# Decode attention over a key and value cache: scores of both batches in one group of products, keys loaded a head ahead of values

## The chip, the core and the metric

The kernel runs on one core of a Trainium2 chip. The core has a matrix engine (TensorE, PE in the profile, with PEld for its weight loads), a vector engine (VectorE, DVE), an activation engine (ScalarE, ACT), GpSimd (POOL) and a sync engine (SyncE, SP), which issues every DMA of this kernel. Each engine takes its own instructions in order, and engines wait for one another through semaphores. The metric is the device time of one execution in microseconds (us). Lower is better.

## The reference, cut to what matters

A transformer block decodes one token for each of two batches, with `D` = 512. Everything is float32. The attention reads only the last 4096 rows of a cache of 32768; eight key and value heads serve 32 query heads, four to a head.

```python
def _A_ref(x, k_cache, v_cache, wq, wo):          # x (2, 1, 512); caches (2, 8, 32768, 128)
    W = min(4096, max(256, Sk // 4))              # 4096
    q = (x @ wq).reshape(B, Sq, Hq, Dh).transpose(0, 2, 1, 3)
    k = repeat(k_cache[:, :, Sk - W:, :], 4, axis=1)
    v = repeat(v_cache[:, :, Sk - W:, :], 4, axis=1)
    scores = einsum("bhqd,bhkd->bhqk", q, k) * Dh ** -0.5
    p = softmax(scores)
    o = einsum("bhqk,bhkd->bhqd", p, v)
    return o.transpose(0, 2, 1, 3).reshape(B, Sq, Hq * Dh) @ wo

def reference(...):
    sa, ca, ga, sb, cb, gb = silu(c) @ w_mod, cut in six
    h = layernorm(x) * (1 + ca) + sa
    x = x + ga * _A_ref(h, A_k_cache, A_v_cache, A_wq, A_wo)
    h = layernorm(x) * (1 + cb) + sb
    x = x + gb * (silu(h @ w1) @ w2)              # w1 (512, 1792), w2 (1792, 512)
```

## The kernel before, in words

All large inputs come in through one ring of eight tiles of 128 x 4096 floats (`RING = 8`, `stream`). A load can be issued once the tile eight loads earlier has been read for the last time. The loads stand on SP's queue in program order: `w_mod` (4 loads), `wq` (4), then for each of eight heads the keys of both batches and the values of both batches (`load_k`, `load_v`, 2 MB each), then `wo` (4), `w1` (3) and `w2` (5).

The loop over heads is a software pipeline, and its order is fixed by hand: each instruction in it is wrapped in `inorder`. For head h, VectorE transposes the keys in 32 x 32 blocks, eight instructions, four for each batch (`keys`). TensorE then multiplies the transposed keys by the queries (`scores`). A product here yields 32 rows of the result, so it occupies a strip of 32 of the array's 128 columns, a column group; the four groups are partitions 0, 32, 64 and 96 of the PSUM bank. Batch 0 uses groups 0 and 1, batch 1 uses groups 2 and 3, and the batches are two separate calls. The program shows each float32 product as two instructions in the trace.

Then `maxima` takes the row maxima (VectorE `mx`, a turn on TensorE `mT`, VectorE `mg` and `mrow`), and `exponentials` sends the bias through TensorE (`bp`) and ScalarE (`bias`), and ScalarE computes the exponentials `pr`. `turn` brings the probabilities into the form of weights: VectorE transposes (`xp`) and masks (`zp`), TensorE multiplies by an identity (`pT`), ScalarE copies to `ptb`. `weighted` multiplies them by the values of both batches, sixteen products over four column groups that accumulate in one bank `o`, which ScalarE copies to `ob`. `collect` adds the head's rows to `o_all`.

In the loop (lines 445 to 467), the turn, the values' products and the collection of head h-1 stand inside the iteration of head h: the first key transpose of h, `turn(h-1)`, the rest of batch 0's transposes, `weighted(h-1)`, `scores(h, 0)`, `collect(h-1)`, batch 1's transposes, `scores(h, 1)`, `maxima(h)`, `exponentials(h)`. At the top of iteration h, `fetch(h+1)` issues the two key loads and then the two value loads of head h+1. The buffers for transposed keys (`kT`) are two, one for each batch.

After the loop the attention's result is normalised (`on`, `oq`, `oTn`), multiplied by `wo` (`acc_o` for 24 of 32 slices, `ao` for the last eight), and the second half of the block follows: the layer norm, `hid` with `w1`, the activation up to `uT`, `acc_yw` and `acc_y` with `w2`, `yo`, and the store.

Of the kernel before, what the change touches and what calls it, by code (L numbers as in the profile page):

```python
# [8 lines left out]
F32 = mybir.dt.float32  # L9
# [4 lines left out]
P = 128  # L14
B, D = 2, 512
HQ, HKV, DH = 32, 8, 128
# [7 lines left out]
def adaln_block(  # L24
# [21 lines left out]
    nc = tc.nc  # L46
# [12 lines left out]
    once = ctx.enter_context(tc.tile_pool(name="once", bufs=1))  # L59
# [3 lines left out]
    def const(shape, name):  # L63
        return consts.tile(shape, F32, name=name)

    def bank(tag, name):
        return (psum1 if tag in "CO" else psum).tile([P, 512], F32, tag=tag, name=name)

    def stream(name):
        return ring.tile([P, 4096], F32, tag="st", name=name)  # L70
# [6 lines left out]
    def load_k(b, h):  # L77
        t = stream(f"k{h}_{b}")
        nc.sync.dma_start(
            t, k_cache[b, h, SK - W :, :].rearrange("(p n) d -> p (n d)", p=P)  # L80
        )
        return t

    def load_v(b, h):
        t = stream(f"v{h}_{b}")
        nc.sync.dma_start(
            t, v_cache[b, h, SK - W :, :].rearrange("(p n) d -> p (n d)", p=P)
        )
        return t
# [93 lines left out]
    ptb = [const([P, 17 * 32], f"ptb{i}") for i in range(2)]  # L183
# [4 lines left out]
    qbd = [const([P, 4, B, 4, 32], f"qbd{n}") for n in range(2)]  # L188
# [52 lines left out]
    for k in range(4):  # L241
        ab = wm[k][:, : 2 * D].rearrange("p (s k a c) -> p a s k c", s=2, k=4, a=4)
        cd = wm[k][:, 2 * D :].rearrange("p (s g m) -> p g s m", s=4, g=4)
        for g in range(4):
            r = slice(32 * g, 32 * g + 32)
            nc.tensor.matmul(m_ch[r, :], scT[:, k, :], ab[:, g], start=(k == 0), stop=(k == 3))
        for g in range(4):
            r = slice(32 * g, 32 * g + 32)
# [19 lines left out]
    def turned(t, name):  # L268
        o = const([P, 4, 32], name)
        nc.vector.transpose(o, t.rearrange("p (m k) -> p k m", k=4))  # L270
        return o
# [9 lines left out]
    for k in range(4):  # L281
        wv = wqt[k].rearrange("p (n s g m) -> p n g s m", n=2, s=4, g=G)
        for n in range(2):
            for g in range(G):
# [4 lines left out]
                    start=(k == 0),  # L289
                    stop=(k == 3),  # L290
                )
    for n in range(2):
        qT = once.tile([P, D], F32, tag="wide", name=f"qT{n}").rearrange("p (s j r) -> p s j r", s=4, r=32)
        nc.vector.transpose(qT.rearrange("p s j r -> p (s j r)"), q_ps[n])  # L294
        for g in range(G):
            r = slice(32 * g, 32 * g + 32)
# [8 lines left out]
        for i in range(4):  # L305
            r = slice(32 * i, 32 * i + 32)
# [10 lines left out]

    inorder = tc.keep_in_program_order
    kt, vt, wot, kT = {}, {}, [], {}
    s_ps, mT, pr, o_sb = {}, {}, {}, {}

    def fetch(h):
        for b in range(B):
            kt[h, b] = load_k(b, h)
        for b in range(B):
            vt[h, b] = load_v(b, h)

    def keys(h, b, n4):

        if n4 == 0:
            kT[h, b] = ktp.tile([P, 4, 32, 32], F32, tag="kT", name=f"kT{h}_{b}")
        inorder(nc.vector.transpose(  # L335
            kT[h, b][:, :, 8 * n4 : 8 * n4 + 8, :].rearrange("p j n k -> p n j k"),
            kt[h, b][:, n4 * 1024 : (n4 + 1) * 1024].rearrange("p (n j r) -> p n j r", j=4, r=32),
        ))

    def scores(h, b):  # L340

        if b == 0:
            s_ps[h] = bank("A", f"s{h}")
        for j in range(4):
            for c in range(2):
                r = 64 * b + 32 * c
                inorder(nc.tensor.matmul(  # L347
                    s_ps[h][r : r + 32, :],
                    qbd[h // 4][:, h % 4, b, j, :],
                    kT[h, b][:, j, 16 * c : 16 * c + 16, :],  # L350
                    start=(j == 0),
                    stop=(j == 3),
                ))

    def maxima(h):
        mx = work.tile([P, 1], F32, tag="mx", name=f"mx{h}")
        inorder(nc.vector.tensor_reduce(mx, s_ps[h], axis=AX.X, op=ALU.max))  # L357
        mT = bank("B", f"mT{h}")
        inorder(nc.tensor.matmul(mT[0:1, :P], mx, ident, start=True, stop=True))  # L359
        m = mrow[h % 2]  # L360
        mg = work.tile([1, B, G], F32, tag="mg", name=f"mg{h}")
        inorder(nc.vector.tensor_reduce(
            mg,
            mT[0:1, :P].rearrange("o (b c i g) -> o b g c i", b=B, c=2, g=G)[:, :, :, :, 0:4],
            axis=AX.XY,
            op=ALU.max,
        ))
        inorder(nc.vector.tensor_copy(  # L368
            m.rearrange("o (b c i g) -> o b c i g", b=B, c=2, g=G)[:, :, :, 0:4, :],
            mg[:, :, None, None, :].to_broadcast([1, B, 2, 4, G]),  # L370
        ))

    def exponentials(h):
        bp = bank("B", f"bp{h}")
        inorder(nc.tensor.matmul(bp[:, 0:1], mrow[h % 2], negscale, start=True, stop=True))  # L375
        bias = work.tile([P, 1], F32, tag="bias", name=f"bias{h}")
        inorder(nc.scalar.copy(bias, bp[:, 0:1]))  # L377
        pr[h] = once.tile([P, 16, 32], F32, tag="pr", name=f"pr{h}")
        inorder(nc.scalar.activation(  # L379
            pr[h].rearrange("p s k -> p (s k)"),  # L380
            s_ps[h],
            AF.Exp,
            bias=bias,
            scale=SCALE,
            accum_out=rowsum[:, h : h + 1],
        ))

    def turn(h):

        xp = once.tile([P, 16, 32], F32, tag="xp", name=f"xp{h}")  # L390
        inorder(nc.vector.transpose(xp, pr[h]))  # L391
        zp = once.tile([P, 4, 16, 16], F32, tag="zp", name=f"zp{h}")
        inorder(nc.vector.tensor_mul(  # L393
            zp,
            xp[:, None, :, 0:16].to_broadcast([P, 4, 16, 16]),
            group[:, :, None, None].to_broadcast([P, 4, 16, 16]),
        ))
        tp = bank("C", f"pT{h}")[:, : 2 * P]
        for i in range(4):
            inorder(nc.tensor.matmul(  # L400
                tp[32 * i : 32 * i + 32, :],
                id4,
                zp.rearrange("p a s x -> p (a s) x")[:, :, 4 * i : 4 * i + 4],
                start=True,
                stop=True,
            ))
        inorder(nc.scalar.copy(  # L407
            ptb[h % 2]
            .rearrange("p (b y) -> p b y", b=B)[:, :, :256]
            .rearrange("p b (w z) -> p b w z", z=32)[:, :, :, 0:16],  # L410
            tp.rearrange("p (b w z) -> p b w z", b=B, z=16),
        ))

    def weighted(h):


        o_ps = bank("D", f"o{h}")
        for b in range(B):
            for w in range(8):
                c = w % 4  # L420
                inorder(nc.tensor.matmul(  # L421
                    o_ps[32 * c : 32 * c + 32, :],
                    ptb[h % 2][:, 256 * b + 32 * w : 256 * b + 32 * w + 32],
                    vt[h, b][:, 512 * w : 512 * w + 512],
                    start=(b == 0 and w < 4),
                    stop=(b == 1 and w >= 4),
                ))
        o_sb[h] = once.tile([P, 4 * DH], F32, tag="wide", name=f"ob{h}")
        inorder(nc.scalar.copy(o_sb[h], o_ps))  # L429

    def collect(h):

        for m in range(4):
            r = 64 * (m % 2)
            inorder(nc.tensor.matmul(  # L435
                o_all[r : r + 64, :],
                selh[:, m, HQ - G - G * h : 3 * HQ - G - G * h],
                o_sb[h][:, m * DH : (m + 1) * DH],
                start=(h == 0 and m < 2),
                stop=(h == HKV - 1 and m >= 2),  # L440
                skip_group_check=True,
            ))

    fetch(0)
    for h in range(HKV + 1):
        last, now = h > 0, h < HKV
        if now:
            if h + 1 < HKV:
                fetch(h + 1)
            keys(h, 0, 0)  # L450
        if last:
            turn(h - 1)
        if now:
            for n4 in range(1, 4):
                keys(h, 0, n4)
        if last:
            weighted(h - 1)
        if now:
            scores(h, 0)
        if last:  # L460
            collect(h - 1)
        if now:
            for n4 in range(4):
                keys(h, 1, n4)
            scores(h, 1)
            maxima(h)
            exponentials(h)

    gaT, sbT, cbT = turned(ga, "gaT"), turned(sb, "sbT"), turned(cb1, "cbT")
    nc.vector.tensor_copy(hT[:, :, 1:32:16], sbT[:, :, 0:32:16])  # L470
# [24 lines left out]
    for r in (0, 64):  # L495
# [4 lines left out]
            start=True,  # L500
            stop=True,
# [33 lines left out]
    for q in range(24):  # L535
# [5 lines left out]
            start=(q < 4),  # L541
            stop=(q >= 20),
        )
    for q in range(24, 32):
        for g in range(4):
# [4 lines left out]
                start=(q == 24),  # L550
                stop=(q == 31),
# [24 lines left out]
    for k in range(4):  # L576
        for g in range(4):
# [4 lines left out]
                start=(k == 0),  # L582
                stop=(k == 3),
# [25 lines left out]
    for tt in range(WIDE):  # L609
# [5 lines left out]
            start=(tt < 4),  # L615
            stop=(tt >= WIDE - 4),
        )
    y = bank("D", "acc_y")[:, :P]
    for tt in range(WIDE, T2):
        for g in range(4):  # L620
# [4 lines left out]
                start=(tt == WIDE),  # L625
                stop=(tt == T2 - 1),
# [35 lines left out]
```

## Time and profile before

| What | us |
| --- | --- |
| median of 3 runs | 246.33 (245.33 to 247.42) |
| the profiled execution, its own time | 246.29 |
| its span, first to last instruction | 244.4 |
| PE busy | 165.3 (68%) |
| PEld busy | 47.4 (19%) |
| DVE busy | 114.7 (47%) |
| ACT busy | 25.4 (10%) |
| mean granted TensorE clock | 0.839 |
| moved by DMA | 97.69 MB, mean 400 GB/s |

The profiled execution's own time is 1.89 us more than its span and agrees with the median to 0.04 us. The page cuts the span in 40 slices and gives each engine's busy share, the granted clock (`PEclk`) and the busy share of the 16 DMA engines. The chain of waits goes back from the last instruction, at each step to what released it; its rows are start, duration, engine, tile and line. A window row gives, for a stretch of time, the busy time of each engine, the clock, the DMA share and GB/s. In the timeline `x7` means seven instructions merged into one row. In the groups a line gives the count, busy time, mean ns and what ended the idle time before them.

### The profile page before, as it was taken

Reading aid. Unit: us, or ns where it says so; the run is one execution under the profiler, and the core shown is the slowest. Engines: PE = TensorE matmul, PEld = TensorE weight load, DVE = VectorE, ACT = ScalarE, POOL = GpSimd, SP = SyncE. Lnnn points to the kernel's source line nnn. Section 1 sums busy time; section 2 is a strip of 40 time slices with the busy share of each in tenths; the row PEclk is TensorE's granted clock in tenths of the full one; section 3 lists DMA queues with packets and bytes.
Section 4 is the critical chain, followed back from the end, with each engine's and each line's share of the span. In section 5 each row is a group of like instructions: output and inputs, shape, how many; then the busy total and the mean of one; then the engine's idle time right before and its main releaser. Section 6 shows DMA issues by size and latency. Waiting matters only on the chain.

```text
span 244.4 us, 2546 instructions
## 1 busy us (share of the span) xinstructions
PE 165.3 (68%) x1048; PEld 47.4 (19%) x1048; DVE 114.7 (47%) x176; ACT 25.4 (10%) x56; POOL 10.3 (4%) x30
## 2 busy tenths in 40 slices
PE   0185655295199479749939938974993994769754
PEld 0131001011022012112202202211220221123312
DVE  0724003781691594397089059339708903110230
ACT  2200000101100100010010010001001001001310
POOL 9500001000000000000000000000000000000000
PEclk9999579679569959967985995997798599589979
DMA  6999999999999999999999999999999999999700
GB/s 254 425 432 437 434 426 429 430 429 434 432 429 426 429 429 432 434 429 429 432 432 429 429 437 429 429 434 434 429 432 429 429 425 432 430 416 390 286 3 1
DMA packets 7603, 97.69 MB, mean 400 GB/s; under 512 B 920, under 2 KB 936, under 8 KB 1576
## 3 DMA queue, kind: packets, MB, share of 16 engines
q1 hardware_dynamic: 7592, 97.54, 94.0%
q8 instruction: 8, 0.13, 0.2%
q14 instruction: 3, 0.02, 0.0%
HBM read 97.53 MB, written 0.00 MB: 399 GB/s over the span
## 4 chain that ended last, share of the span: by engine, by line
PE 56%; DMA 24%; DVE 11%; ACT 4%; issue 3%
PE s L347 20%; PE o L421 20%; DMA k<-in_A_k_cache_dram 15%; DMA wq<-in_A_wq_dram 6%; DVE zp L393 4%; PE pT L400 4%; DMA wm<-in_w_mod_dram 3%; DVE xp L391 2%; ACT pr L379 2%; PE acc_o L537 2%; DVE mx L357 2%; PE o_all L435 2%; PE acc_yw L611 1%; PE hid L578 1%; ACT ptb L407 1%
## 5 line engine op out<-in xcount | busy, mean ns | idle before, releaser
L335 DVE STREAM_TRANSPOSE kT<-k 128x1024 f32<-128x1024 f32 x64 | 73.7, 1211 | 3.8 <-DMA k<-in_A_k_cache_dram 3.8
L347 PE MATMUL s<-kT,qbd 128*32 128x512 f32 x256 | 60.6, 604 | 3.8 <-DVE kT L335 3.7
L421 PE MATMUL o<-v,ptb 128*32 128x512 f32 x256 | 47.8, 914 | 3.9 <-ACT ptb L407 3.9
L357 DVE TENSOR_REDUCE mx<-s 128x1 f32<-128x512 f32 x8 | 5.5, 691 | 55.2 <-PE s L347 55.2
L400 PE MATMUL pT<-zp,id 128*32 128x256 f32 x64 | 8.6, 630 | 26.3 <-DVE zp L393 26.3
L347 PEld LDWEIGHTS s<-kT,qbd 128*32 128x32 f32 x256 | 14.2, 111 | 43.0 <-issue 36.4
L421 PEld LDWEIGHTS o<-v,ptb 128*32 128x32 f32 x256 | 10.4, 159 | 41.0 <-issue 30.1
L285 PE MATMUL q<-wq,hq_T 128*32 128x512 f32 x64 | 11.6, 859 | 8.8 <-DMA wq<-in_A_wq_dram 8.8
L393 DVE TENSOR_TENSOR zp<-xp,group 128x1024 f32<-128x1024 f32 x8 | 9.8, 1225 | 0.2
L294 DVE STREAM_TRANSPOSE qT<-q 128x512 f32<-128x512 f32 x2 | 1.4, 718 | 18.1 <-PE q L285 17.8
L429 ACT COPY ob<-o 128x512 f32<-128x512 f32 x8 | 4.7, 585 | 48.9 <-PE o L421 48.9
L377 ACT COPY bias<-bp 128x1 f32<-128x1 f32 x8 | 1.3, 159 | 77.7 <-PE bp L375 77.7
L217 PE MATMUL mean_a<-mv_a,avg 128*128 128x1 f32 x2 | 0.6, 362 | 10.6 <-DVE mv_a L214 10.6
L359 PE MATMUL mT<-ident,mx 128*1 128x128 f32 x16 | 3.0, 270 | 6.3 <-DVE mx L357 6.3
L391 DVE STREAM_TRANSPOSE xp<-pr 128x512 f32<-128x512 f32 x8 | 5.7, 706 | 3.3 <-ACT pr L379 3.3
L400 PEld LDWEIGHTS pT<-zp,id 128*32 128x32 f32 x64 | 1.8, 140 | 26.8 <-issue 25.9
L407 ACT COPY ptb<-pT 128x256 f32<-128x256 f32 x8 | 3.0, 372 | 28.4 <-PE pT L400 28.4
L375 PE MATMUL bp<-negscale,mrow 1*128 1x1 f32 x16 | 3.0, 256 | 4.2 <-DVE mrow L368 4.2
L435 PE MATMUL o_all<-ob,selh 128*64 128x128 f32 x64 | 5.3, 285 | 0.7 <-ACT ob L429 0.7
L285 PEld LDWEIGHTS q<-wq,hq_T 128*32 128x32 f32 x64 | 2.1, 129 | 18.3 <-DMA wq<-in_A_wq_dram 11.2
L537 PE MATMUL acc_o<-wo,oTn 128*32 128x512 f32 x48 | 5.4, 594 | 0.4 <-DVE oTn L515 0.4
L379 ACT ACTIVATE pr<-s,bias 128x512 f32<-128x512 f32 x8 | 5.5, 687 | 0.2
(130 smaller groups left out, 89.7 us busy)
## 6 DMA issues: line engine op xcount, KB each, us to landing
k<-in_A_k_cache_dram SPq DMA_DIRECT2D x16, 2048.0 KB, 31.4
v<-in_A_v_cache_dram SPq DMA_DIRECT2D x16, 2048.0 KB, 23.5
wq<-in_A_wq_dram SPq DMA_DIRECT2D x4, 2048.0 KB
wo<-in_A_wo_dram SPq DMA_DIRECT2D x4, 2048.0 KB, 20.5
wm<-in_w_mod_dram SPq DMA_DIRECT2D x4, 1536.0 KB, 10.2
w<-in_B_w_dram SPq DMA_DIRECT2D x2, 1024.0 KB, 5.9
w<-in_B_w_dram SPq DMA_DIRECT2D x1, 1792.0 KB
w<-in_B_w_dram SPq DMA_DIRECT2D x2, 896.0 KB
```

The source lines that it names most:

```text
L285: nc.tensor.matmul(q_ps[n][32 * g : 32 * g + 32, :], hq_T[:, k, :], wv[:, n, g], start=(k == 0), stop=(k == 3),)
L335: inorder(nc.vector.transpose(kT[h, b][:, :, 8 * n4 : 8 * n4 + 8, :].rearrange("p j n k -> p n j k"), kt[h, b][:, n4 * 1024 : (n4 + 1) * 1 ...
L347: inorder(nc.tensor.matmul(s_ps[h][r : r + 32, :], qbd[h // 4][:, h % 4, b, j, :], kT[h, b][:, j, 16 * c : 16 * c + 16, :], start=(j == 0) ...
L357: inorder(nc.vector.tensor_reduce(mx, s_ps[h], axis=AX.X, op=ALU.max))
L379: inorder(nc.scalar.activation(pr[h].rearrange("p s k -> p (s k)"), s_ps[h], AF.Exp, bias=bias, scale=SCALE, accum_out=rowsum[:, h : h + 1],))
L391: inorder(nc.vector.transpose(xp, pr[h]))
L393: inorder(nc.vector.tensor_mul(zp, xp[:, None, :, 0:16].to_broadcast([P, 4, 16, 16]), group[:, :, None, None].to_broadcast([P, 4, 16, 16]),))
L400: inorder(nc.tensor.matmul(tp[32 * i : 32 * i + 32, :], id4, zp.rearrange("p a s x -> p (a s) x")[:, :, 4 * i : 4 * i + 4], start=True, st ...
L407: inorder(nc.scalar.copy(ptb[h % 2] .rearrange("p (b y) -> p b y", b=B)[:, :, :256] .rearrange("p b (w z) -> p b w z", z=32)[:, :, :, 0:16 ...
L421: inorder(nc.tensor.matmul(o_ps[32 * c : 32 * c + 32, :], ptb[h % 2][:, 256 * b + 32 * w : 256 * b + 32 * w + 32], vt[h, b][:, 512 * w : 5 ...
L435: inorder(nc.tensor.matmul(o_all[r : r + 64, :], selh[:, m, HQ - G - G * h : 3 * HQ - G - G * h], o_sb[h][:, m * DH : (m + 1) * DH], start ...
L537: nc.tensor.matmul(acc[32 * g : 32 * g + 32, :], oTn[:, q, :], wot[q // 8][:, q % 8, :], start=(q < 4), stop=(q >= 20),)
```

## The change

Three things are different.

- `fetch(h)` now issues the keys of head h and the values of head h-1. Keys of head h+1 therefore stand ahead of the values of head h in SP's queue; before the loop only the keys of head 0 are issued, and the last call, `fetch(8)`, issues the values of head 7 alone. The number of loads and their sizes are the same.
- `scores(h)` is one call for both batches, after all eight key transposes. Its loop goes over j, then batch, then half, so four neighbouring products go to four column groups. The products themselves are the same 16.
- `weighted` is called once for each batch. Batch 0's eight products stand ahead of the scores of the next head, batch 1's behind its exponentials. `collect` follows one iteration later, right behind `turn`.

```diff
     def fetch(h):
-        for b in range(B):
-            kt[h, b] = load_k(b, h)
-        for b in range(B):
-            vt[h, b] = load_v(b, h)
+        if h < HKV:
+            for b in range(B):
+                kt[h, b] = load_k(b, h)
+        if h > 0:
+            for b in range(B):
+                vt[h - 1, b] = load_v(b, h - 1)
...
-    def scores(h, b):
-        if b == 0:
-            s_ps[h] = bank("A", f"s{h}")
+    def scores(h):
+        s_ps[h] = bank("A", f"s{h}")
         for j in range(4):
-            for c in range(2):
-                r = 64 * b + 32 * c
+            for b in range(B):
+                for c in range(2):
+                    r = 64 * b + 32 * c
...
-    def weighted(h):
-        o_ps = bank("D", f"o{h}")
-        for b in range(B):
-            for w in range(8):
+    def weighted(h, b):
+        if b == 0:
+            o_ps[h] = bank("D", f"o{h}")
+        for w in range(8):
...
-        o_sb[h] = once.tile([P, 4 * DH], F32, tag="wide", name=f"ob{h}")
-        inorder(nc.scalar.copy(o_sb[h], o_ps))
+        if b == 1:
+            o_sb[h] = once.tile([P, 4 * DH], F32, tag="wide", name=f"ob{h}")
+            inorder(nc.scalar.copy(o_sb[h], o_ps[h]))
...
         if now:
-            if h + 1 < HKV:
-                fetch(h + 1)
+            fetch(h + 1)
             keys(h, 0, 0)
         if last:
             turn(h - 1)
+        if h > 1:
+            collect(h - 2)
+        if last:
+            weighted(h - 1, 0)
         if now:
-            for n4 in range(1, 4):
-                keys(h, 0, n4)
-        if last:
-            weighted(h - 1)
-        if now:
-            scores(h, 0)
-        if last:
-            collect(h - 1)
-        if now:
-            for n4 in range(4):
-                keys(h, 1, n4)
-            scores(h, 1)
+            for n in range(1, 8):
+                keys(h, n // 4, n % 4)
+            scores(h)
             maxima(h)
             exponentials(h)
+        if last:
+            weighted(h - 1, 1)
+    collect(HKV - 1)
```

TensorE's queue before, from the turn of head 1 to the maxima of head 2. `o_467` is the values' sum of head 1, `s_486` the scores of head 2, `kT_0` and `kT_1` the transposed keys of the two batches, `o_all` the collection.

```order
-L400 MATMUL pT_458<-zp_456,id_58 32x256 x4
-L421 MATMUL o_467<-v_0_319,ptb_154 32x512 x8
-L421 MATMUL o_467<-v_1_321,ptb_154 32x512 x8
-L347 MATMUL s_486<-kT_0_452,qbd_159 32x512 x8
-L435 MATMUL o_all<-ob_484,selh 64x128 x4
-L347 MATMUL s_486<-kT_1_499,qbd_159 32x512 x8
-L359 MATMUL mT_514<-ident,mx_512 1x128
```

The same place now: `o_460` is the values' sum of head 1, `s_477` the scores of head 2.

```order
+L402 MATMUL pT_450<-zp_448,id_58 32x256 x4
+L438 MATMUL o_all<-ob_434,selh 64x128 x4
+L423 MATMUL o_460<-v_0_363,ptb_154 32x512 x8
+L349 MATMUL s_477<-kT_0_444,qbd_159 32x512 x2
+L349 MATMUL s_477<-kT_1_472,qbd_159 32x512 x2
...
+L361 MATMUL mT_496<-ident,mx_494 1x128
+L377 MATMUL bp_501<-negscale,mrow_151 128x1
+L423 MATMUL o_460<-v_1_365,ptb_154 32x512 x8
+L402 MATMUL pT_531<-zp_529,id_58 32x256 x4
```

Batch 1's products with the values have moved from ahead of the scores to the place between `bp` and the next `pT`; the collection is that of head 0 and has moved from between the two scores to behind `pT`. The order of VectorE's instructions is unchanged.

SP's queue from the second head's keys on, before and now (the numbers behind the names only tell tiles apart):

```order
 L79 DMA k_0_307<-in_A_k_cache_dram 128x4096
 L79 DMA k_1_309<-in_A_k_cache_dram 128x4096
-L86 DMA v_0_311<-in_A_v_cache_dram 128x4096
-L86 DMA v_1_313<-in_A_v_cache_dram 128x4096
-L79 DMA k_0_315<-in_A_k_cache_dram 128x4096
-L79 DMA k_1_317<-in_A_k_cache_dram 128x4096
...
+L79 DMA k_0_311<-in_A_k_cache_dram 128x4096
+L79 DMA k_1_313<-in_A_k_cache_dram 128x4096
+L86 DMA v_0_315<-in_A_v_cache_dram 128x4096
+L86 DMA v_1_317<-in_A_v_cache_dram 128x4096
```

The first two rows are the keys of head 0. Behind them stood the values of head 0; now the keys of head 1 stand there, and the values of head 0 behind those.

More of the change, by code (lines that the diff above doesn't have):

```diff
@@ L322, in adaln_block @@
     kt, vt, wot, kT = {}, {}, [], {}
-    s_ps, mT, pr, o_sb = {}, {}, {}, {}
+    s_ps, pr, o_ps, o_sb = {}, {}, {}, {}
     def fetch(h):
-        for b in range(B):
-            kt[h, b] = load_k(b, h)
-        for b in range(B):
-            vt[h, b] = load_v(b, h)
+        if h < HKV:
[4 more added lines that the diff above has]
+                vt[h - 1, b] = load_v(b, h - 1)
     def keys(h, b, n4):
@@ L338, in keys @@
         ))
-    def scores(h, b):
-        if b == 0:
-            s_ps[h] = bank("A", f"s{h}")
+    def scores(h):
+        s_ps[h] = bank("A", f"s{h}")
         for j in range(4):
-            for c in range(2):
-                r = 64 * b + 32 * c
[L347 to L353, printed above, removed]
+            for b in range(B):
+                for c in range(2):
+                    r = 64 * b + 32 * c
+                    inorder(nc.tensor.matmul(
+                        s_ps[h][r : r + 32, :],
+                        qbd[h // 4][:, h % 4, b, j, :],
+                        kT[h, b][:, j, 16 * c : 16 * c + 16, :],
+                        start=(j == 0),
+                        stop=(j == 3),
+                    ))
     def maxima(h):
@@ L412, in turn @@
         ))
-    def weighted(h):
-        o_ps = bank("D", f"o{h}")
-        for b in range(B):
-            for w in range(8):
[L420 to L427, printed above, removed]
-        o_sb[h] = once.tile([P, 4 * DH], F32, tag="wide", name=f"ob{h}")
-        inorder(nc.scalar.copy(o_sb[h], o_ps))
+    def weighted(h, b):
+        if b == 0:
+            o_ps[h] = bank("D", f"o{h}")
+        for w in range(8):
+            c = w % 4
+            inorder(nc.tensor.matmul(
+                o_ps[h][32 * c : 32 * c + 32, :],
+                ptb[h % 2][:, 256 * b + 32 * w : 256 * b + 32 * w + 32],
+                vt[h, b][:, 512 * w : 512 * w + 512],
+                start=(b == 0 and w < 4),
+                stop=(b == 1 and w >= 4),
+            ))
+        if b == 1:
+            o_sb[h] = once.tile([P, 4 * DH], F32, tag="wide", name=f"ob{h}")
+            inorder(nc.scalar.copy(o_sb[h], o_ps[h]))
     def collect(h):
```

## The prediction

> **What bounds the kernel now.** I read the page's slices first, then the chain of waits.
>
> ```profile
> DMA  6999999999999999999999999999999999999700
> ```
>
> The DMA engines are full until the 38th of 40 slices (6.1 us each) and then empty while the kernel runs on for two slices and a half. Something other than DMA sets the end. The chain shows what, here one head in its middle, then the end:
>
> ```profile
> 25.79 37.46 DMA k<-in_A_k_cache_dram
> 63.27 1.25 DVE kT L335
> ...
> 183.03 0.70 DVE mx L357
> ...
> 184.69 0.39 PE bp L375 x2
> ...
> 185.29 0.79 ACT pr L379 x2
> 186.10 0.72 DVE xp L391
> 186.85 1.24 DVE zp L393
> 188.22 1.11 PE pT L400 x8
> 189.35 0.38 ACT ptb L407
> 189.78 6.11 PE o L421 x32
> 195.89 3.43 PE s L347 x16
> 199.31 0.59 PE o_all L435 x8
> 199.90 3.58 PE s L347 x16
> 203.50 0.70 DVE mx L357
> ...
> 210.17 6.21 PE o L421 x32
> 216.40 0.59 ACT ob L429
> ...
> 219.93 5.36 PE acc_o L537 x48
> 225.29 0.87 PE ao L546 x32
> ...
> 229.41 1.71 PE hid L578 x16
> ...
> 233.12 2.49 issue
> 235.61 3.56 PE acc_yw L611 x16
> ...
> 240.33 0.70 PE acc_y L621 x24
> ...
> 241.38 0.29 DVE yo L632
> ```
>
> From 63.27, where the first keys of head 1 land, no DMA is on the chain. A head costs 203.50 - 183.03 = 20.47 us, end to end through four engines: 5.06 from `mx` to the end of `zp`, 1.70 to the values' products, 6.11 for them, 7.60 for the scores with the collection between. What does DMA need for a head?
>
> ```profile
> 63.27:222.10 158.83, 118.89 (x668) 32.32 (x672) 88.09 (x100) 14.22 (x37) 0.00 (x0) 0.82 1.01 430
> ```
>
> The last number is 430 GB/s. A key or value load is 4096 x 128 floats, 2.097 MB: 4.88 us each, 19.5 us for a head's four. So the chain falls almost 1 us behind per head, the ring hides it, and the debt comes due at the end. The fifth key or value load landed at 63.27; the last, the 32nd, follows 27 x 4.88 = 131.7 later, at 195.0. Its products start at 210.17, 15 us late, and everything behind them with it.
>
> **The loads.** The change keeps the number and bytes of the loads. Ahead of the last values stand the same 31 loads, so they again land at 195.0. Values of an earlier head land later by two loads, 9.8 us: head 0's at 63.3 and 68.1, where their products before ran from 68.1. At nothing, then, while TensorE arrives no earlier; if it does, it waits, and DMA sets the pace. The ring's part: the loads of head h's values can be issued once batch 1's products of head h-2 are done, later than before, and every later load queues behind them on SP. Eight loads, 39.0 us, lie between the landings of the two; to keep the DMA engines full the issue must come 9.8 us ahead of that for the loads themselves, so 29 us behind the landing of head h-2's values. Even at half clock the products are done 16.4 us behind it (3.6 for batch 0's, 7.1 for the scores, 2.1 from `mx` to the end of `bp`, 3.6 for batch 1's; the rows follow). Some 12 us remain, less the lag. Cost zero; if that cover is gone, each microsecond costs one.
>
> **The head.** What stands between the end of one head's scores and the next? VectorE's order is unchanged, but TensorE's part is not. Values' products of batch 1 leave the stretch from `ptb` to the scores and go behind `bp`; there TensorE had nothing to do until `pT` (185.08 to 188.22), 3.1 us, and the eight products (16 instructions) need 1.8 to 3.6. So they come at nothing at full clock, at 0.5 us at half. They now wait for a load in TensorE's queue ahead of `pT`, and on ScalarE the copy `ob` (0.59) waits for them between `pr` and `ptb`; if batch 1's values are late, the whole next turn stands behind them, microsecond for microsecond. The collection (0.6) goes into the 0.4 us in which TensorE waits for `ptb`; its rest is covered by the transposes. With batch 1's products gone, VectorE is late next:
>
> ```profile
> 45.08 9.13 DVE L335 STREAM_TRANSPOSE kT<-k 128x1024 f32<-128x1024 f32 x8
> 187.99 8.00 DVE L335 STREAM_TRANSPOSE kT<-k 128x1024 f32<-128x1024 f32 x7
> ```
>
> The scores of both batches now need all eight transposes. The last seven end 8.00 us behind `zp`, at 195.99, 12.96 after `mx`'s start. TensorE does its `pT`, collection and batch 0's products within these eight (1.11 + 0.4 + 0.6 + at most 3.6). So a head is 12.96 plus the scores. For the scores the row of 48 instructions over four column groups, 5.36, gives 0.112 us each at full clock, and the row of 16 in 3.56 at half clock 0.222. The two-group scores took 3.43/16 = 0.214 at full clock, so four groups halve it. 32 instructions: 3.6 us at full, 7.1 at half. The head then takes 16.6 or 20.1 us, against 20.47 before and DMA's 19.5. **At full clock DMA becomes the bound; at half clock the gain is a third of a microsecond.** The clock decides. The next rows are windows cut where the granted clock was seen to change, all multiples of 3.41 us apart; the columns are busy time of PE, PEld, DVE, ACT and POOL, then clock, DMA share and GB/s:
>
> ```profile
> 184.56:187.97 3.41, 0.38 (x2) 0.29 (x2) 3.06 (x4) 0.94 (x3) 0.00 (x0) 1.00 1.00 428
> 187.97:191.39 3.42, 2.69 (x16) 0.63 (x20) 3.42 (x4) 0.37 (x1) 0.00 (x0) 0.50 0.98 422
> 191.39:194.80 3.41, 3.41 (x20) 0.79 (x16) 3.41 (x5) 0.00 (x0) 0.00 (x0) 0.50 1.03 442
> 194.80:198.21 3.41, 3.41 (x24) 0.92 (x18) 1.18 (x2) 0.58 (x1) 0.00 (x0) 1.00 0.99 416
> 215.28:218.69 3.41, 1.89 (x22) 0.76 (x15) 0.61 (x2) 0.58 (x1) 0.00 (x0) 1.00 0.96 404
> 218.69:222.11 3.42, 3.06 (x30) 1.43 (x33) 0.54 (x2) 0.00 (x0) 0.00 (x0) 1.00 1.03 432
> ```
>
> The number behind each length is TensorE's busy time. A window with 0.38 is followed by half clock, one with 1.89 is not, and half clock ends only behind a window that is nearly full (2.69 was not enough). That is why 32 value instructions took 6.11: the wait for the softmax had put the clock down. Now that wait holds batch 1's products: 0.4 + 0.4 + 1.8 busy within 5.1 us, near 1.89 in a window, so the clock should stay up. The Trainium skill (TensorE: Matmul & The Clock Gate, HAM oscillation) says that an idle stretch longer than about 3.4 us puts the clock to half, and that a kernel that waits for loads falls into this at every tile. On the step the trace agrees (0.38 busy, then 0.50). By that rule each head that waits for its values would pay the half-clock price, which is the first rival's sum.
>
> I take DMA's pace, 19.5, with the clock going down in some heads: at 16.6, a head waits up to 2.9 us for values, which with the idle stretch around it can drop the clock; the next products lose up to 3.4 us and use up the wait, and a late head does not wait. It limits itself, and I carry a lag of 0 to 3.5 us.
>
> The start: the eight transposes of head 0 end at 54.2; the scores then take 3.6 to 7.1, where the two-group scores, begun while the transposes ran, were over here:
>
> ```profile
> 57.93 0.69 DVE L357 TENSOR_REDUCE mx<-s 128x1 f32<-128x512 f32 x1 [3.71 <-PE s L347]
> ```
>
> That loses up to 3.4, against a gain, since the transpose ahead of `xp` no longer waits until 63.27. The 3 us of slack in each head absorb it by head 2.
>
> **The end.** Values of head 6, batch 0, land at 195.0 - 3 x 4.88 = 180.4. Batch 0's products 1.8 to 3.6, scores 3.6 to 7.1, 5.1 to `zp`, 1.7 to the next products: 192.6 to 197.9. The last head's 32 instructions, the last 16 not before 195.0, end at 198 to 205, against 216.38 before. From there to `acc_o` it took 219.93 - 216.38 = 3.55: 201 to 209. But `wo` comes at DMA's pace, four loads like the others: the last lands at 195.0 + 19.5 = 214.5. So DMA is late next, and the earlier `wo` products hide behind it. `w1` (3584 KB, 3.67 MB) lands by 223.1 and `w2` (as much) by 231.6, if the queue stays full. Before, it did not:
>
> ```profile
> 225.35 2.39 SPq L95 DMA_DIRECT2D w<-in_B_w_dram  x2
> 226.00:227.00 1.00, 1.00 (x44) 0.95 (x40) 0.00 (x0) 0.99 (x1) 0.00 (x0) 1.00 0.83 270
> 230.00:231.00 1.00, 1.00 (x12) 0.13 (x4) 0.00 (x0) 0.00 (x0) 0.00 (x0) 1.00 0.92 358
> ```
>
> Pieces of `w2` waited for `wo`'s tiles to come free; now those are free by 218, long before their turn. At 370 GB/s, as in such rows, `w2` needs 9.9 instead of 8.5 and lands at 233. TensorE's own chain from `ao`, 214.5: 4.1 to `hid` (229.41 - 225.29), at half clock about 6; `hid` (1.71 and as much again, 3.4; at half 6.8) ends no earlier than 224.0 for `w1`, no later than 227.3; 2.5 to `acc_yw`; that 1.8 to 3.6; `acc_y` as before in 1.9 (241.03 - 239.17). That makes 230.2 to 235.2, not before the last load, 231.9. From the end of `acc_y` (240.33 + 0.70; `yo` and the store follow) to the span's end of 244.4 there are 3.4 us: 235.3 to 238.6. I take 236.6, since in such waits the clock will sometimes be down. With the 1.9 us around the span: **238.5 us**, 237 to 241 in this case, against 246.29 for the profiled execution, which stands within 0.04 of the median.
>
> **Rivals.** *Half clock throughout.* Every head at 20.1. For it: the scores begin behind a wait for transposes, and 2.69 busy was not enough to bring the clock up. Against: the value products now fill the wait. Seven heads save 7 x 0.37 = 2.6, and the start loses 0 to 3.4: 243.7 to 247.1, say 245.4. Chance 0.13.
>
> *DMA is the bound already.* Its share is 9 in every slice. The Trainium skill (Perfetto Trace Analysis, Identifying the Most-Contended Engine) advises to find the engine with the highest occupancy and optimize this first; the change leaves it alone. The trace speaks against that reading: 15 us lie between the last values and their products. If it held: 246. Chance 0.02.
>
> *Slower: four groups do not overlap when keys of two batches stream.* TensorE's scores are the place. If each instruction keeps 0.214 us, the scores take 6.8 at full and 13.7 at half clock, behind all transposes: 19.8 or 26.7 per head. It decides from 7.5 us for the scores (20.47 - 12.96). At half of each, 23.2, seven heads lose 19: 265. Against: the value products and `acc_o` already reach 0.112 over four groups with four different streams. Chance 0.06.
>
> **Numbers.** The forecast has 0.79, from 237 to 241; of it perhaps 0.04 lies below 236. The range 236 to 244 holds it and part of the half-clock case. About 1% (2.5 us) is what can be told from no change: faster 0.80, with a little of the first rival; same 0.13, the rest of it and the second; slower 0.07, the third and the first's upper edge.
>
> **What would show it.** Right: a period of 19.5 from one `mx` to the next, DMA rows for values or `wo` on the chain, the values' products of head 7 done by 205, the last 16 scores instructions near 0.11 us each. Wrong: a period of 20 with PEclk 0.50 over the scores; scores above 7 us; holes in the DMA row; or, if the heads come out right and the end does not, `hid` and `acc_yw` at half clock beyond what I allowed.

## The result and the profile after

| | before | changed |
| --- | --- | --- |
| median, us | 246.14 (4 runs, 245.33 to 247.42) | 238.14 (4 runs, 237.08 to 238.53) |
| ratio to before | | 0.9664, 95% interval 0.9611 to 0.9717 |
| profiled execution: its time, its span | 246.29, 244.4 | 237.97, 236.1 |
| mean granted TensorE clock | 0.839 | 0.834 |

The change saves 8 us, 3.4%. Two kernels below (the new order of loads alone, two of ten executions; the scores done twice, three of ten) had executions more than 1.5% above their fastest, and their medians and ratios leave these out. In the page's slices the DMA engines are now busy to within one slice (5.9 us) of the end:

```profile
DMA  6999999999999999999999999999999999999990
```

The chain of waits of the changed kernel, with start, duration, engine, tile and line, at two heads in the first half, then at one in the second and at the end:

```profile
82.07 7.92 DVE kT L337 x7
90.00 0.04 issue
90.04 5.33 PE s L349 x26
...
95.39 0.70 DVE mx L359
...
100.43 7.92 DVE kT L337 x7
108.36 0.04 issue
108.40 3.63 PE s L349 x26
...
112.06 0.70 DVE mx L359
...
125.45 34.98 DMA v<-in_A_v_cache_dram
160.44 0.14 issue
160.57 3.64 PE o L423 x16
164.22 4.24 PE s L349 x32
...
181.45 32.51 DMA wo<-in_A_wo_dram
213.96 0.04 issue
214.00 1.93 PE ao L546 x32
...
222.76 2.14 PE hid L578 x16
...
227.40 3.47 PE acc_yw L611 x16
...
232.01 0.70 PE acc_y L621 x24
```

Until 125 the chain runs from the end of `zp` through seven key transposes, then the scores, then the maxima. From there on it is DMA, with one head's work between: values until 160.44, then `wo` until 213.96, and TensorE's own steps at the end. Before the change no DMA stood on it behind 63.27. The groups of waits of TensorE say the same; a row gives the total, the count and the longest wait:

```profile
PE o L423 <- DMA v<-in_A_v_cache_dram: 18.8, 5, 5.3
PE s L349 <- DVE kT L337: 11.2, 9, 3.4
PE acc_o L537 <- DMA wo<-in_A_wo_dram: 3.6, 2, 3.0
```

The maxima of heads 2 to 7, from the timeline (start, duration, and in brackets how long VectorE was idle before):

```profile
95.39 0.69 DVE L359 TENSOR_REDUCE mx<-s 128x1 f32<-128x512 f32 x1 [5.41 <-PE s L349]
112.06 0.69 DVE L359 TENSOR_REDUCE mx<-s 128x1 f32<-128x512 f32 x1 [3.71 <-PE s L349]
128.72 0.69 DVE L359 TENSOR_REDUCE mx<-s 128x1 f32<-128x512 f32 x1 [3.71 <-PE s L349]
148.52 0.69 DVE L359 TENSOR_REDUCE mx<-s 128x1 f32<-128x512 f32 x1 [6.17 <-PE s L349]
168.48 0.69 DVE L359 TENSOR_REDUCE mx<-s 128x1 f32<-128x512 f32 x1 [6.69 <-PE s L349]
186.75 0.69 DVE L359 TENSOR_REDUCE mx<-s 128x1 f32<-128x512 f32 x1 [5.32 <-PE s L349]
```

Two heads in a row take 16.67 us, the chain by itself. Then the heads have caught up with their values and take 19.8 and 19.96; the last one, its scores wholly at full clock, takes 18.3. From head 4's iteration on batch 0's products with the values (here of heads 3 to 6) begin when their load has landed; in brackets stands how long TensorE waited:

```profile
121.68 3.38 PE L423 MATMUL o<-v,ptb 128*32 128x512 f32 x16 [3.22 <-DMA v<-in_A_v_cache_dram]
141.13 3.64 PE L423 MATMUL o<-v,ptb 128*32 128x512 f32 x16 [4.67 <-DMA v<-in_A_v_cache_dram]
160.57 3.64 PE L423 MATMUL o<-v,ptb 128*32 128x512 f32 x16 [5.32 <-DMA v<-in_A_v_cache_dram]
180.03 3.22 PE L423 MATMUL o<-v,ptb 128*32 128x512 f32 x16 [5.15 <-DMA v<-in_A_v_cache_dram]
```

They are 19.44 to 19.46 us apart, which is DMA's pace. Head 7's maxima come at 186.75 where they came at 203.50.

### The profile page after: what moved, and what is told of

Its sections match the earlier page's. It is cut to its first block, busy times and chain, and to the rows that moved or that the text cites. A ratio compares the mean times of both kernels' runs of the same rounds, so it can differ in the third digit from the quotient of the medians.

```text
span 236.1 us, 2552 instructions
## 1 busy us (share of the span) xinstructions
PE 142.1 (60%) x1048; PEld 43.8 (19%) x1048; DVE 114.8 (49%) x176; ACT 25.4 (11%) x56; POOL 10.3 (4%) x30
## 4 chain that ended last, share of the span: by engine, by line
DMA 44%; DVE 30%; PE 20%; ACT 3%; issue 1%; SPq 1%; DVEq 0%; ACTq 0%
DVE kT L337 21%; DMA v<-in_A_v_cache_dram 15%; DMA wo<-in_A_wo_dram 14%; DMA wq<-in_A_wq_dram 13%; PE s L349 9%; DMA wm<-in_w_mod_dram 3%; DVE zp L395 3%; PE hid L578 2%; ACT pr L381 2%; PE q L285 2%; PE o L423 2%; DVE xp L393 2%; DVE mx L359 1%; PE acc_yw L611 1%; PE ao L546 1%
## 5 line engine op out<-in xcount | busy, mean ns | idle before, releaser
L349 PE MATMUL s<-kT,qbd 128*32 128x512 f32 x256 | 43.4, 649 | 11.2 <-DVE kT L337 11.2
L423 PE MATMUL o<-v,ptb 128*32 128x512 f32 x256 | 38.2, 727 | 19.3 <-DMA v<-in_A_v_cache_dram 18.8
L349 PEld LDWEIGHTS s<-kT,qbd 128*32 128x32 f32 x256 | 11.5, 121 | 44.0 <-DVE kT L337 21.5
L423 PEld LDWEIGHTS o<-v,ptb 128*32 128x32 f32 x256 | 8.1, 124 | 35.3 <-issue 32.2
L402 PE MATMUL pT<-zp,id 128*32 128x256 f32 x64 | 5.7, 429 | 14.1 <-DVE zp L395 14.1
L537 PE MATMUL acc_o<-wo,oTn 128*32 128x512 f32 x48 | 8.1, 811 | 4.0 <-DMA wo<-in_A_wo_dram 3.6
L294 DVE STREAM_TRANSPOSE qT<-q 128x512 f32<-128x512 f32 x2 | 1.4, 717 | 18.4 <-PE q L285 18.4
L249 PE MATMUL m_sp<-wm,scT 128*32 128x512 f32 x32 | 5.9, 824 | 0.0
L285 PEld LDWEIGHTS q<-wq,hq_T 128*32 128x32 f32 x64 | 2.1, 133 | 18.3 <-DMA wq<-in_A_wq_dram 12.0
```

Of the source, the lines that this page charges most:

```text
L249: nc.tensor.matmul(m_sp[r, :], scT[:, k, :], cd[:, g], start=(k == 0), stop=(k == 3))
L285: nc.tensor.matmul(q_ps[n][32 * g : 32 * g + 32, :], hq_T[:, k, :], wv[:, n, g], start=(k == 0), stop=(k == 3),)
L349: inorder(nc.tensor.matmul(s_ps[h][r : r + 32, :], qbd[h // 4][:, h % 4, b, j, :], kT[h, b][:, j, 16 * c : 16 * c + 16, :], start=(j == 0) ...
L402: inorder(nc.tensor.matmul(tp[32 * i : 32 * i + 32, :], id4, zp.rearrange("p a s x -> p (a s) x")[:, :, 4 * i : 4 * i + 4], start=True, st ...
L423: inorder(nc.tensor.matmul(o_ps[h][32 * c : 32 * c + 32, :], ptb[h % 2][:, 256 * b + 32 * w : 256 * b + 32 * w + 32], vt[h, b][:, 512 * w ...
L537: nc.tensor.matmul(acc[32 * g : 32 * g + 32, :], oTn[:, q, :], wot[q // 8][:, q % 8, :], start=(q < 4), stop=(q >= 20),)
```

## The experiments

Two theories were set against each other. **Pace**: a head takes the longer of DMA's 19.5 us and its chain through the engines; TensorE's part of the change brings the chain below DMA's, and there the gain ends. **Shares**: the three parts of the change (order of loads, scores over four groups, split of the values' products) each bring some of the 8 us. Six kernels make up, with the kernel before and the changed one, all eight combinations of the three parts.

| loads | scores | split | median, us | ratio to before, 95% interval |
| --- | --- | --- | --- | --- |
| old | old | old | 245.97 and 246.25 beside these runs | 1 |
| new | old | old | 243.44 | 0.9908 (0.9864 to 0.9952) |
| old | new | old | 237.19 | 0.9644 (0.9596 to 0.9692) |
| old | old | new | 237.34 | 0.9656 (0.9604 to 0.9708) |
| old | new | new | 237.34 | 0.9654 (0.9591 to 0.9717) |
| new | old | new | 236.96 | 0.9639 (0.9572 to 0.9705) |
| new | new | old | 238.02 | 0.9683 (0.9601 to 0.9765) |
| new | new | new | 238.14, measured apart | 0.9664 (0.9611 to 0.9717) |

### The order of loads alone

```diff
     def fetch(h):
-        for b in range(B):
-            kt[h, b] = load_k(b, h)
-        for b in range(B):
-            vt[h, b] = load_v(b, h)
+        if h < HKV:
+            for b in range(B):
+                kt[h, b] = load_k(b, h)
+        if h > 0:
+            for b in range(B):
+                vt[h - 1, b] = load_v(b, h - 1)
...
         if now:
-            if h + 1 < HKV:
-                fetch(h + 1)
+            fetch(h + 1)
```

> The kernel before with the new order of loads alone. Two theories. Pace: a head takes the longer of DMA's 19.5 us and the chain through the engines, and only TensorE's part of the change shortens the chain. Shares: the three parts each bring some of the 8 us. Pace expects a head of 20.4 us as before and 244 to 246; up to 2 us come off at the start, since the turn of head 0 no longer waits for the keys of head 1 at 63.3. Shares expects about 243.5, a third of the gain.

243.44 us, a gain of 0.9% that the interval keeps apart from none. The time alone does not decide: it is the 243.5 that shares expected, and half a microsecond below pace's range. The trace speaks for pace. Its execution took 244.98. Head 1's maxima come at 80.09 instead of 81.22, since the turn of head 0 no longer stands behind keys that land at 63.27; the heads after that take 20.1 to 20.5 us, as before, and head 7's maxima come 1.35 us earlier (202.15 against 203.50). So what the trace shows of the gain lies mostly at the start, and no head has come down to DMA's 19.5. The next two kernels separate the theories by their times.

### The scores alone

```diff
# scores(h) with its loop as in the change; in the loop over heads:
...
-        if now:
-            for n4 in range(1, 4):
-                keys(h, 0, n4)
         if last:
             weighted(h - 1)
         if now:
-            scores(h, 0)
+            for n in range(1, 8):
+                keys(h, n // 4, n % 4)
+            scores(h)
         if last:
             collect(h - 1)
         if now:
-            for n4 in range(4):
-                keys(h, 1, n4)
-            scores(h, 1)
...
```

Here `weighted(h - 1)` stays whole, ahead of `scores(h)`, and `collect(h - 1)` follows behind the scores.

> The kernel before with the scores of both batches in one call over four column groups, the values' products unsplit ahead of them, the loads in the old order. Pace: the chain of a head is 5.1 + 1.7 + 6.1 for the values' products + 3.6 for the scores = 16.5 us, below DMA's 19.5, so this part alone gives the whole gain: 237 to 240. If the clock stays at half for the scores too: 20.0, 244 to 246. Shares: 241 to 243.

237.19 us: the whole gain from one part. From head 1 on the maxima are 19.4 to 19.9 us apart, DMA's pace, and 53% of the span on the chain is loads of keys. `oTn`, the attention's normalised result, begins at 210.59, where the kernel before has 219.61.

### The split alone

```diff
# weighted(h, b) as in the change; in the loop over heads:
...
         if last:
             turn(h - 1)
+        if h > 1:
+            collect(h - 2)
+        if last:
+            weighted(h - 1, 0)
...
-        if last:
-            weighted(h - 1)
...
-        if last:
-            collect(h - 1)
...
             exponentials(h)
+        if last:
+            weighted(h - 1, 1)
+    collect(HKV - 1)
```

> The kernel before with the values' products split around the scores and the collection a head later, the scores in two calls over two column groups each, the loads in the old order. Pace: after the last key transpose, 13.0 us behind the maxima, only batch 1's scores are left, 3.5 us at full clock: 16.5 us, below 19.5, so this part alone too gives the whole gain: 237 to 240. Shares: 241 to 243.

237.34 us: the whole gain again, from the other part. From head 1 on the maxima are 19.4 to 19.7 us apart, and 52% of the span on the chain is loads of keys. Two changes that each bring 8 us bring 8 us together, which no sum of shares gives.

### Each part undone

```diff
# the loads, in the changed kernel (fetch as before the change)
...
+            if h + 1 < HKV:
+                fetch(h + 1)
-            fetch(h + 1)
...
# the scores (with the loop of two calls)
...
+            for n4 in range(1, 4):
+                keys(h, 0, n4)
...
+            scores(h, 0)
+            for n4 in range(4):
+                keys(h, 1, n4)
+            scores(h, 1)
-            for n in range(1, 8):
-                keys(h, n // 4, n % 4)
-            scores(h)
...
# the split (with collect(h - 1) behind the scores)
...
+            weighted(h - 1)
...
-            weighted(h - 1, 0)
...
-            weighted(h - 1, 1)
```

> The changed kernel with the old order of loads. Pace: 237 to 240, as the changed kernel, but the waits for DMA stand at VectorE's key transposes where they stood at TensorE's products with the values; the last keys land at 185, their scores end near 194 and the last head is still done before the last load of wo at 214. Shares: 240 to 242, since the loads' share is lost.

> The changed kernel with the scores in two calls over two column groups each. Pace: 13.0 + 3.5 = 16.5 us for a head's chain at full clock, so DMA still sets the pace: 237 to 240. Shares: 240 to 242.

> The changed kernel with the values' products of both batches together ahead of the scores. Pace: 5.1 + 1.7 + 6.1 + 3.6 = 16.5 us for a head's chain: 237 to 240. With half clock in the scores too 20 us and 243 to 246. Shares: 240 to 242.

237.34, 236.96 and 238.02. None of the three can be told from the changed kernel. In each `oTn` begins ahead of the last `wo` tile, which lands near 214 (208.10, 202.83 and 207.18), so the loads still set what follows. Without the new order of loads the wait only moves, to the transposes, as the waits of that kernel show:

```profile
DVE kT L335 <- DMA k<-in_A_k_cache_dram: 21.4, 7, 3.3
```

### More work on the chain

Does the changed kernel have room in its head? The first of two kernels repeats half of the score products of every head, the second all of them.

```diff
+        for js in (range(2), range(4)):        # the second kernel: (range(4), range(4))
-        for j in range(4):
+            for j in js:
...
-                        stop=(j == 3),
+                            stop=(j == js[-1]),
```

> The changed kernel with the first eight of the sixteen score products of each head done once more ahead of all sixteen (the same result is written again): 16 more instructions of 0.112 us, 1.8 us per head, all on the chain. Pace: 16.6 + 1.8 = 18.4 us, still below 19.5, so no change: 237 to 240. If the head's chain still sets the time in the changed kernel, 8 x 1.8 = 14 us more: 252.

> The changed kernel with all sixteen score products of each head done twice: 3.6 us more per head. Pace: 16.6 + 3.6 = 20.2 us, above 19.5; head 7's maxima come near 205, its products with the values end near 216, where they ended before the change, behind the last load of wo at 214: 243 to 246. So the second half of the dose costs 6 us where the first costs nothing. If the chain still sets the time: 8 x 3.6 = 29 us more, 267.

237.74 us (ratio 0.9667, 0.9597 to 0.9737) for the first, 245.49 (ratio 0.9991, 0.9939 to 1.0043) for the second. 16 more instructions in each head cost nothing; the next 16 cost the whole gain. The maxima of the second kernel, heads 3, 4 and 7:

```profile
124.35 0.69 DVE L360 TENSOR_REDUCE mx<-s 128x1 f32<-128x512 f32 x1 [7.15 <-PE s L350]
144.44 0.69 DVE L360 TENSOR_REDUCE mx<-s 128x1 f32<-128x512 f32 x1 [7.15 <-PE s L350]
...
206.27 0.69 DVE L360 TENSOR_REDUCE mx<-s 128x1 f32<-128x512 f32 x1 [7.15 <-PE s L350]
```

20.09 us a head, against 20.2 expected, and the time is in the range given. One head (144.44 to 166.09) took 21.65, part of its scores at half clock, so the last maxima came 1.3 us behind the 205. `oTn` begins at 219.49, where the kernel before has 219.61, and the times are the same. In the first kernel two heads take 18.4 us at full clock, as expected, but four take 19.8 to 20.1, part of their scores at half clock, which the sum had left out. Its `oTn` begins at 209.54, ahead of the last `wo` tile, and its chain ends behind a load of `w2` (231.56): the room is used, and nothing shows outside.

### The chain without the values' loads

```diff
-            vt[h, b] = load_v(b, h)
+            vt[h, b] = load_v(b, h) if h == 0 else vt[0, b]
```

with these two tiles outside the ring and `RING = 6`; the same in the changed kernel.

> The kernel before with the values of head 0 used for all heads (fourteen loads of 2 MB left out; their two tiles lie outside the ring, which has six tiles here). DMA then needs 9.8 us a head and the chain stands alone. Pace: a head still takes 20.4 us and the whole 243 to 246, since DMA did not set it. If DMA set the time before: 73 us less at the most.

> The changed kernel with the values of head 0 used for all heads, as in the run beside it. Pace: a head takes its chain, 16.6 us with the clock up, 18 to 18.5 where the scores begin at half clock, and the whole takes 216 to 226. If DMA was not the bound of the changed kernel: 236 to 239, no change. If the clock falls to half in every head: 20.1 us a head, 241 to 245.

One run of each: 245.37 us for the kernel before, 220.74 for the changed one. With 29 MB fewer to load the kernel before gains nothing (its own runs beside these: 244.34 to 246.10), so DMA did not set its time; the changed kernel falls by another 17 us, so DMA sets that. The last maxima of the changed kernel without the loads:

```profile
146.94 0.69 DVE L360 TENSOR_REDUCE mx<-s 128x1 f32<-128x512 f32 x1 [3.71 <-PE s L350]
163.60 0.69 DVE L360 TENSOR_REDUCE mx<-s 128x1 f32<-128x512 f32 x1 [3.71 <-PE s L350]
180.26 0.69 DVE L360 TENSOR_REDUCE mx<-s 128x1 f32<-128x512 f32 x1 [3.71 <-PE s L350]
```

16.66 us a head is the chain at full clock.

### The clock in the second half

```diff
+    def busy(name, lhsT, rhs, n):
+        d = bank("B", name)
+        for i in range(n):
+            g = i % 4
+            inorder(nc.tensor.matmul(d[32 * g : 32 * g + 32, :], lhsT, rhs, start=True, stop=True))
...
+        if q % 8 == 7:
+            busy(f"fill{q}", oTn[:, q, :], wot[q // 8][:, q % 8, :], 8)
...
+    busy("fill_u", hT[:, 3, :], w1t[3][:, :512], 4)
```

> The changed kernel with products that nobody reads in the waits of the second half: eight behind each of the first three tiles of wo, four behind hid. They should keep TensorE's clock up, so ao, hid and acc_yw take about 1.3, 1.4 and 1.7 us less than in the changed kernel's trace. If the last load sets the end (it lands near 232, and acc_y ends at 232.7): no more than 0.5 us less, 237.3 to 238.5. If TensorE's own chain sets it: 3 to 4 us less, 234 to 235.

237.12 us, ratio 0.9686 (0.9661 to 0.9710), not told from the changed kernel's 0.9664. Its trace has `ao` in 2.18 instead of 3.53 and `acc_yw` in 2.04 instead of 3.42, but `hid` still in 5.05 instead of 5.25: its weight loads wait for tiles of `w1` (0.78 and 1.57 us), and the clock goes down in it. The end of its chain is a load:

```profile
213.97 16.50 DMA w<-in_B_w_dram
230.47 0.04 issue
230.52 1.11 PE acc_y L630 x24
```

The last load lands at 230.47 and `acc_y` ends at 231.63, against 232.71 in the changed kernel, whose last products stood behind TensorE's own chain. So by the traces that chain set the last 1.1 us, more than the 0.5 expected, and DMA the rest; the runs' times are too close to show the 1.1. No version among these beats the changed kernel by more than the runs can tell.

## Why the prediction was right

The forecast was 238.5, measured is 238.14; span 236.6, measured 236.1. The mechanism came out as given: TensorE's chain was the bound, the change brings a head below DMA's 19.5 us, and there the gain ends. That the total is right within half a microsecond is in part luck, as the end of the list shows. Step by step:

- **What bounded the kernel before.** TensorE's chain, not DMA, which carried the debt to the end. The one run without the values' loads shows it: 245.37.
- **The loads at no cost.** Shown for the changed kernel: with the old order it takes 237.34. Alone they bring 0.9%, of which the trace shows 1.35 us, 1.13 of it by head 1's maxima; the sum had named this gain and put it into the heads' slack. The ring's 12 us in hand held; no hole appeared in the DMA row. Landing times came out as worked: values of head 6 at 180.0 (180.4 said), the last `wo` tile at 214.0 (214.5).
- **Batch 1's products behind `bp` at nothing.** The seven begin between 78.99 and 188.70 and take 1.92 us each, all at full clock.
- **The head at 16.6 us at full clock.** 16.66 and 16.67. One term in it was right by another way: the scores were put at 32 instructions of 0.112. Six of them run ahead, as their transposes end, and the other 26 take 3.63, since the last column group gets its first keys with the last transpose and does its eight instructions one behind the other. Eight instructions stand in each group in either kernel: 16 over two groups took 3.43 before, 32 over four take 3.62 in head 7 (183.06). At full clock the two ways of counting come to the same.
- **The clock.** It stays up through the softmax of heads 1 to 7, as forecast, but for the end of head 4's. In heads 1 to 3 and 7 the windows over the softmax hold 2.08 us or more of TensorE's work, above the 1.89 that the prediction counted on. In head 4 VectorE waited 1.03 us for keys ahead of the turn, the window from 131.49 to 134.91 held only 1.43, and the clock went down; TensorE waited for values next, so nothing was lost. The clock goes down in the waits for values, as forecast: the products of heads 3 to 6 shown above take 3.2 to 3.6 us, at half clock. But the step "a late head does not wait" did not come about. All four waited, for 3.2 to 5.3 us where the prediction has up to 2.9. The key transposes go on while TensorE waits (seven of them from 134.36 to 142.35), so they no longer stand between the products and the scores, and the cost of the half clock went into the wait. In head 2 the clock went down for a reason that the prediction gave to its first rival: the gaps in which TensorE waits for transposes. The windows around it, with columns as in the prediction's:

```profile
87.12:90.53 3.41, 1.54 (x10) 0.33 (x14) 2.86 (x3) 0.00 (x0) 0.00 (x0) 1.00 1.02 437
90.53:93.95 3.42, 3.42 (x24) 0.85 (x17) 0.00 (x0) 0.00 (x0) 0.00 (x0) 0.50 1.01 431
...
104.19:107.60 3.41, 1.90 (x8) 0.14 (x2) 3.41 (x4) 0.00 (x0) 0.00 (x0) 1.00 1.01 428
107.60:111.01 3.41, 2.61 (x25) 0.80 (x26) 0.74 (x1) 0.00 (x0) 0.00 (x0) 1.00 1.01 432
```

After the window with 1.54 busy the clock was at half, and that head took 18.36 instead of 16.67; one head later, after 1.90, it was not. The loss did not reach the end, since the values' loads still bounded the later heads. The Trainium skill (TensorE: Matmul & The Clock Gate, HAM oscillation) speaks of an idle stretch of more than about 3.4 us; here the longest in that window was 1.21 us, between two score products, and the clock went down all the same.

- **The lag and the end.** The last value products end at 196.6, ahead of the 198 to 205 given. The 198 was added up wrongly: 192.6 and 3.6 are 196.2, and 1.8 behind the last landing at 195.0 is 196.8. `hid` ends at 224.9 (224.0 to 227.3 said), `acc_y` at 232.7 (230.2 to 235.2). The mis-sized term is the last load. It was worked out as 231.6 with the queue full and 233 at 370 GB/s (the 231.9 in the sum has no working of its own); in the kernel with the busy clock it lands at 230.47, 16.5 us behind the last `wo` tile where the sum had 17.1. TensorE's own chain, with `acc_yw` at half clock (3.42), ended 1.1 us later than `acc_y` behind that load would have (232.71 against 231.63), and the two cancel.
- **The pace came later than said.** By head 2 the head was to wait for values. The first wait of more than 0.5 us is in head 4's iteration, at 121.68, since a head at full clock catches up only 2.8 us, and two took longer: head 1 (17.93), behind a table load of 1.28 us on ScalarE ahead of head 0's exponentials, and head 2 (18.36).

The rivals: half clock throughout did not occur (PEclk 1.00 over the scores of five of eight heads, 0.68 to 0.92 over the others). DMA as the bound already is refuted by the run without the values' loads. The slower one is refuted by head 7's scores: products of four groups with keys of two batches overlap, 32 instructions in 3.62 us, where the rival needed 6.8.

## What to carry to other kernels

When an engine's chain is only slightly slower than the stream of loads, buffers hide the difference and a full DMA row looks like the bound; look at whether the chain of waits has any DMA on it, and at how late the last tile is used after it has landed. What an edit to such a chain is worth is the distance to the next bound. Several edits that each cross it bring no more together than one does, and repeating a part of the work shows the room that is left.

## What the runs showed of the hardware that had not been expected

The busy time of a window does not settle the clock of the next by itself. In the changed kernel 1.84 us of 3.41 was followed by half clock (196.35 to 199.76), 1.90 was not (104.19 to 107.60), which looks like a sharp edge. Other runs cross it: with the split undone, 1.98 and 1.93 were followed by half clock (75.67 to 79.08, 113.21 to 116.63); with all scores twice, 1.64 was not (133.29 to 136.71). Nor is "nearly full" a sharp edge on the way up: 2.66 at half clock was followed by full clock in the changed kernel (179.28 to 182.69), 2.78 was not in the kernel before (208.45 to 211.87). What else counts stays open.

In the kernel before, the head's period creeps up and then stays: 20.18, 20.33, 20.40, 20.44, 20.46, 20.47 us. With the new loads alone it ends at 20.46, and without the values' loads too:

```profile
161.22 0.69 DVE L357 TENSOR_REDUCE mx<-s 128x1 f32<-128x512 f32 x1 [7.44 <-PE s L347]
181.66 0.69 DVE L357 TENSOR_REDUCE mx<-s 128x1 f32<-128x512 f32 x1 [7.49 <-PE s L347]
202.12 0.69 DVE L357 TENSOR_REDUCE mx<-s 128x1 f32<-128x512 f32 x1 [7.51 <-PE s L347]
```

Six windows of 3.413 us (the step between the prediction's windows, 30.72 over nine) are 20.48. In the kernel before, the clock comes up at 153.84, 174.32 and 194.80, and the value products end 1.1 us behind each (154.96, 175.42, 195.89), so the head seems to fall in step with the windows. This is argued from three kernels and not shown; no run tried it by itself. If it holds, small savings in such a head may give nothing until they reach the next window.
